# Transposing the softmax weights as 32-bit words on the matrix engine of a cached attention kernel

## The chip, the cores and the metric

The kernel runs on one core of a Trainium2 chip. A core has a matrix engine (TensorE, PE in the profile, with its weight loads shown apart as PEld), a vector engine (VectorE, DVE), a scalar engine (ScalarE, ACT), GpSimd (POOL) and a sync engine (SyncE, SP), which here only issues DMAs. Each engine works through its own list of instructions in order; engines wait for one another on semaphores. Matrix results land in PSUM (eight banks of 128 partitions by 512 fp32 words), everything else lies in SBUF. The metric is the device time of one execution, in microseconds. The kernel before takes 455.86 us, the median of three runs.

## What is computed

```python
B, Sq, D = 8, 112, 640
H, Sk, Dh = 32, 512, 192
q = (x @ wq).reshape(B, Sq, H, Dh).transpose(0, 2, 1, 3)
scores = einsum("bhqd,bhkd->bhqk", q, k_cache) * Dh ** -0.5
p = softmax(scores, axis=-1)
o = einsum("bhqk,bhkd->bhqd", p, v_cache)
out = o.transpose(0, 2, 1, 3).reshape(B, Sq, H * Dh) @ wo
```

All inputs are bf16. There are 8 x 32 = 256 pairs of a batch entry and a head; each has a 112 x 512 score matrix, and p of each has to be turned round (keys on partitions) before it can be multiplied with v.

## The kernel before, in words

A **step** n treats four heads of one batch entry; there are 64 steps, numbered 0 to 63. `t = n // 4` is a pair of half (16 heads) and batch entry. In step n the matrix engine computes scores for n (`scores`, the matmuls named `Sm` and `St`, lines 368 to 383, into banks 0 to 3), multiplies p with v for step n-2 (`values`, `PVt` line 459 and `PVm` line 470, banks 4 and 5), does a share of the query projection for a later step (`q_fill`, line 313: `Qa` is 10 matmuls of 224 columns into bank 6, `Qb` is 5), a share of the output projection of an earlier group of heads (`o_half`, line 504, bank 7: 12 matmuls of 224 columns for one block of outputs, 24 for two), and transposes p of step n-1 (`transposes`, line 431, `PT`, 8 transposes into bank 4 and 8 into bank 5).

The softmax of one head: DVE scales and negates the scores from PSUM into `s_sb` and takes the row minimum at once (`smax`, line 396; `s_sb` has two slots, so the third `smax` of a step waits for the first `exp`), ACT exponentiates into `p_sb` with the row sum (`exp`, line 401), DVE inverts two row sums (`rc`, line 413) and scales p (`norm`, line 405). After the transposes of step n-1, ACT copies bank 4 and DVE copies bank 5 to `pT_sb` (`evPT`, line 437). ACT also copies the result of p times v (`evPV`, line 480) and the projected queries (`evQa` and `evQb`, line 319). DVE also copies queries to a second layout (`qc`, lines 345 and 346) and adds the output projection to its sum (`oacc`, lines 520 and 522).

The order on every engine is written out by hand: a loop over n from 4 to 57 (lines 732 to 773) appends the operations of each step to the lists `pe`, `act` and `dve`, and lists at the start and the end (`go`, `TAIL`) do so for the rest. `Plan.run` emits each list in order and waits on a semaphore only for those dependencies that the engine has not yet seen. What sets the start of an operation is thus its place in the list of its engine, and the dependencies given to `add`. A dependency that matters here is made in `fill`: the first operation that writes a PSUM bank waits for the copy that last emptied it, so `PT(n-1)` waits for `evPV(n-2)`, since both use banks 4 and 5.

In step n the lists are:

- PE: scores(n), p times v (n-2), `Qa`, output projection part 0, `PT(n-1)`, output projection part 1, `Qb`. With one block of outputs, part 0 has 8 of 12 matmuls; with two blocks 12 of 24. Where a step has no query projection (n = 18 and 19, "light"), all but the last matmul count as part 0 and both parts lie ahead of `PT`.
- ACT: `exp` 0, `exp` 1, `evPV(n-2)`, `exp` 2, `evQa`, `exp` 3, `evPT(n-1, 0)`, `evQb`.
- DVE: `smax` 0 to 3, `rc` 0, `norm` 0 and 1, `qc(n+1)`, `evPT(n-1, 1)`, `oacc`, `rc` 1, `norm` 2 and 3. In light steps `qc` lies after `smax` 1.

The output projection goes round in four steps: n = 16, 20, 24, ... has one block, 17, 21, 25, ... two, the next two one each. Steps 9, 10, 13 and 14 have such shares too, steps 11 and 15 two shares each; steps 4 to 8 and 12 have none. Steps 57 to 61 get their p turned round by DMA (`BY_DMA`, line 418) and not on PE; `transposes` is used for 59 steps.

On SP one list issues all loads: for each t, k by a transposing DMA (line 150, waits for the scores of t-2), v for the second eight heads of t-1 (line 165, waits until its buffer has been used), weights now and then (`wo` at line 208, `wq` at line 198), v for the first eight heads of t.

Of the kernel before, what the change touches and what calls it, by code (L numbers as in the profile page):

```python
# [11 lines left out]
class Plan:  # L12
# [7 lines left out]
    def add(self, eng, name, deps, emit, sem=None, inc=1):  # L20
        assert name not in self.ops, name
        self.ops[name] = dict(eng=eng, deps=deps, emit=emit, sem=sem or eng, inc=inc)

    def number(self):
        self.count = {}
        for eng, names in self.order.items():
            for n in names:
                o = self.ops[n]
                o["at"] = {}
                for s in o["sem"] if isinstance(o["sem"], tuple) else (o["sem"],):  # L30
                    self.count[s] = self.count.get(s, 0) + o["inc"]
                    o["at"][s] = self.count[s]
        assert sum(map(len, self.order.values())) == len(self.ops)

    def run(self, eng_name, eng, sems):
        seen = {}
        for n in self.order[eng_name]:
            o = self.ops[n]
            need = {}
            for d in o["deps"]:  # L40
                if d in self.ops:
                    for s, v in self.ops[d]["at"].items():
                        need[s] = max(need.get(s, 0), v)
            for s, v in need.items():
                if seen.get(s, 0) < v:
                    eng.wait_ge(sems[s], v)
                    seen[s] = v
            last = o["emit"](eng)
            for ins, s in zip(last if isinstance(last, tuple) else (last,), o["at"]):
                ins.then_inc(sems[s], o["inc"])  # L50


def build_mha_kernel(nc, x, k_cache, v_cache, wq, wo, out):
# [27 lines left out]
    with ExitStack() as es:  # L81
# [15 lines left out]
        ident = sb("ident", [128, 128], BF16)  # L97
        nmx = sb("nmx", [SQ, 8], F32)
# [206 lines left out]
        def q_fill(m, lp, part, bank):  # L305
            half, bp = divmod(m, B // 2)
            blocks = (0, 1) if part == "a" else (2,)

            def emit(e):
                for j, c in enumerate(blocks):  # L310
                    for dc in range(DC):
                        c0 = lp * 2 * DH + 128 * c
                        mm = e.matmul(ps[:, bank, j * S2:(j + 1) * S2], wq_sb[:, dc, c0:c0 + 128],  # L313
                                      xT_sb[:, dc, bp * S2:(bp + 1) * S2], start=(dc == 0), stop=(dc == DC - 1))
                return mm

            def evac(e):
                n = len(blocks)
                return e.activation(q_home(m, lp)[:, blocks[0]:blocks[0] + n, :],  # L319
                                    ps[:, bank, 0:n * S2].rearrange("p (c s) -> p c s", c=n), ACTF.Copy)  # L320

            old = []
            if m != 1 and q_seq.index((m, lp)) >= NQ:
                for n in q_last(*q_seq[q_seq.index((m, lp)) - NQ]):
                    old += [("St", n, 3), ("qc", n)]
            rows = range(bp * S2 // 128, (bp * S2 + S2 - 1) // 128 + 1)
            add("PE", ("Q" + part, m, lp), [wq_piece[half, lp]] + [("evX", c) for c in rows], emit)
            add("ACT", ("evQ" + part, m, lp), [("Q" + part, m, lp)] + old, evac)
# [59 lines left out]
        def softmax(n):  # L388
            for i in range(4):
                j, h = divmod(i, 2)  # L390
                k = (4 * n + i) % 8
                a = (4 * n + i) % NSS
                old = divmod(4 * n + i - NSS, 4)

                def smax(e, j=j, h=h, k=k, a=a):
                    return e.tensor_scalar(s_sb[:, a, :].rearrange("p (e c) -> p e c", e=2),  # L396
                                           ps[0:SQ, 2 * j:2 * j + 2, h * 256:(h + 1) * 256], -scale, None,
                                           op0=ALU.mult, op1=ALU.min, accum_out=nmx[:, k:k + 1])

                def exp(e, k=k, a=a):  # L400
                    return e.activation(p_sb[:, k, :], s_sb[:, a, :], ACTF.Exp, bias=nmx[:, k:k + 1], scale=-1.0,  # L401
                                        accum_out=rsum[:, k:k + 1])

                def norm(e, k=k):
                    return e.tensor_scalar(p_sb[:, k, :], p_sb[:, k, :], rinv[:, k:k + 1], None, op0=ALU.mult)  # L405
                add("DVE", ("smax", n, i), [("St", n, 2 * j + 1), ("exp", *old)], smax)
                add("ACT", ("exp", n, i), [("smax", n, i), ("TD", n - 2) if n - 2 in BY_DMA else ("PT", n - 2, j)], exp)
                add("DVE", ("norm", n, i), [("rc", n, j)], norm)
# [15 lines left out]
        def transposes(n, j):  # L424
            bank = end_bank.get(("PT", n, j), 4 + j)

            def emit(e):
                for h in range(2):
                    for q in range(4):
                        c = (4 * h + q) * SQ  # L430
                        mm = e.transpose(psb[:, bank, c:c + SQ], p_sb[:, (4 * n + 2 * j + h) % 8, q * 128:(q + 1) * 128],  # L431
                                         ident[0:SQ, 0:SQ])
                return mm

            def evac(e):
# [3 lines left out]
                ([("smax", n, i) for i in range(4)] if n == NN - 1 else []), emit)  # L439
            add("DVE" if j else "ACT", ("evPT", n, j), [("PT", n, j)] + ([] if n - 1 in BY_DMA else [("PVm", n - 1, j)]), evac)  # L440

        def values(n):
# [5 lines left out]
            def pT(j, h, q):  # L448
# [3 lines left out]
                return pT_sb[:, j, h, q * SQ:(q + 1) * SQ]  # L452
# [32 lines left out]
        FILLS = [(0,), (1, 2), (3,), (4,)]  # L485
        KU = KB // 2
# [8 lines left out]
        def o_half(u, f, part):  # L495
# [3 lines left out]
            cut = len(todo) - 1 if (u, f) in whole else 2 * KU // 3 if len(blocks) == 1 else KU  # L499
            todo = todo[:cut] if part == 0 else todo[cut:]  # L500

            def emit(e):
                for j, m, k in todo:
                    mm = e.matmul(ps[:, o_bank(u, f), j * S2:(j + 1) * S2], wo_sb[:, KU * (u % 2) + k, m * 128:(m + 1) * 128],  # L504
                                  oT_sb[:, u % NO, k, :], start=(k == 0), stop=(k == KU - 1))
                return mm
# [3 lines left out]
            add("PE", ("O", u, f, part), deps, emit)  # L510
# [101 lines left out]
        whole = [o for n, os_ in o_at.items() for o in os_ if n not in q_at]  # L612
# [31 lines left out]
        holder = {}  # L644

        def fill(op, bank, evac, first=True):

            if op not in pe:
# [83 lines left out]
        for n in range(4, END):  # L732
# [3 lines left out]
            s_pe(n)  # L736
            late = any((place(n + 1)[0] // 2, 2 * place(n + 1)[1] + j) in qs for j in range(2))
# [9 lines left out]
            for o in os_[:1]:  # L747
                o_pe(o, 0)
                if two or light:
                    o_pe(o, 1)  # L750
            pt_pe(n - 1)
# [3 lines left out]
            elif os_ and not light:  # L755
                o_pe(os_[0], 1)
            b_q = []
            for g in qs:
                if os_:
                    q_pe(g, "b", 6)  # L760
                b_q.append(("evQb", *g))

# [6 lines left out]
            dve += [("qc", n + 1)] if not late and not early else []  # L769
            dve += [("evPT", n - 1, 1)]  # L770
            dve += [("oacc", *o) for o in (os_[1:2] if two else os_[:1])]
            dve += [("rc", n, 1), ("norm", n, 2), ("norm", n, 3)]
# [45 lines left out]
        def _(e):  # L818
            e.wait_ge(gINIT, 1)
# [20 lines left out]
        def _(e):  # L840
# [3 lines left out]
                            pattern=[[-1, 128]], channel_multiplier=1).then_inc(gINIT, 1)  # L844
    return nc
# [40 lines left out]
```

## Time and profile before

| what | value |
|---|---|
| time, median of 3 runs (lowest, highest) | 455.86 us (455.81, 456.63) |
| profiled execution, first to last instruction | 456.1 us |
| PE busy | 432.3 us, 95% |
| DVE busy | 364.6 us, 80% |
| ACT busy | 334.1 us, 73% |
| POOL busy | 0.7 us |
| mean granted clock of PE | 0.993 |
| transposes of p on PE | 944, busy 57.2 us |

For the profiled execution the page gives its span, from the first to the last instruction, and no other time; that span is 0.24 us above the median of the runs and lies between their lowest and highest. In a line of the profile the engine and the line of the code are followed by what is written, `<-`, and what is read. Brackets at the end of a line give the idle time of the engine ahead of it and who ended it. "x16" is a count of like instructions taken together; the time beside them then runs from the first start to the last end. A matmul's own length holds its way through the array, so the pace of a row of them is read from start to start.

### The profile page before, as it was taken

What the parts mean: (1) busy time and instruction counts of PE and PEld (TensorE: products, weight loads), DVE (VectorE), ACT (ScalarE), POOL (GpSimd) and SP (SyncE); (2) the same over time, 40 slices, a digit from 0 to 9 for tenths busy, and PEclk for the clock granted to TensorE, in tenths of its full rate; (3) what the DMA queues carried; (4) which work ended last, traced back from release to release, by engine and by line L of the source; (5) the groups of instructions that cost most, each with busy time, mean ns of one, the idle gap of its engine ahead of it and who ended that gap; (6) DMA issues with size and microseconds to landing.
All of it is one profiled execution on the core that took longest, in us unless ns stands there. A gap on an engine that the chain in (4) does not pass through costs nothing.

```text
span 456.1 us, 14769 instructions
## 1 busy us (share of the span) xinstructions
PE 432.3 (95%) x6227; PEld 398.1 (87%) x6227; DVE 364.6 (80%) x1160; ACT 334.1 (73%) x782; POOL 0.7 (0%) x6
## 2 busy tenths in 40 slices
PE   5788999999979999999999999997999999999996
PEld 4777888989979899999999999996999999999996
DVE  0577799888868989888888888886688888889971
ACT  3668799867857777877687768776577687767783
POOL 0000000000000000000000000000000000000000
PEclk9999999999999999999999999998899999999999
DMA  8999999999999999999999999999989999999972
GB/s 266 373 363 202 284 244 374 216 314 313 245 317 230 345 230 316 243 293 276 253 319 239 315 228 334 282 235 367 226 225 262 261 213 250 270 225 251 225 204 64
DMA packets 243442, 121.93 MB, mean 267 GB/s; under 512 B 194864, under 2 KB 243376, under 8 KB 243376
## 3 DMA queue, kind: packets, MB, share of 16 engines
q1 hardware_dynamic: 243376, 120.99, 110.0%
q8 instruction: 49, 0.80, 0.7%
q14 instruction: 17, 0.14, 0.1%
HBM read 70.35 MB, written 1.15 MB: 157 GB/s over the span
## 4 chain that ended last, share of the span: by engine, by line
PE 79%; ACT 10%; DMA 6%; DVE 5%; issue 0%; SPq 0%; DVEq 0%
PE ps L504 17%; PE ps L313 16%; PE ps L470 10%; PE ps L431 9%; PE ps L381 7%; ACT p_sb L401 6%; PE ps L459 6%; PE ps L368 6%; PE ps L370 5%; DMA wo_sb<-in_wo_dram 3%; DVE s_sb L396 2%; DMA vt<-in_v_cache_dram 2%; PE ps L543 1%; ACT oT_sb L480 1%; PE ps L567 1%; DVE p_sb L405 1%
## 5 line engine op out<-in xcount | busy, mean ns | idle before, releaser
L401 ACT ACTIVATE p_sb<-s_sb,nmx 112x512 bf16<-112x512 f32 x256 | 182.4, 713 | 83.8 <-DVE s_sb L396 81.8
L396 DVE TENSOR_SCALAR_CACHE_REDUCE s_sb<-ps 112x512 f32<-112x512 f32 x256 | 167.2, 687 | 42.5 <-ACT p_sb L401 20.0
L313 PE MATMUL ps<-xT_sb,wq_sb 128*128 128x224 bf16 x960 | 111.4, 262 | 1.3 <-ACT xT_sb L278 1.3
L504 PE MATMUL ps<-oT_sb,wo_sb 128*128 128x224 bf16 x840 | 97.7, 261 | 3.3 <-DMA wo_sb<-in_wo_dram 3.3
L313 PEld LDWEIGHTS ps<-xT_sb,wq_sb 128*128 128x128 bf16 x960 | 90.2, 99 | 2.8 <-DMA wq_sb<-in_wq_dram 1.1
L405 DVE TENSOR_SCALAR p_sb<-p_sb,rinv 112x512 bf16<-112x512 bf16 x256 | 79.0, 350 | 4.4
L504 PEld LDWEIGHTS ps<-oT_sb,wo_sb 128*128 128x128 bf16 x840 | 78.8, 98 | 3.9 <-DMA wo_sb<-in_wo_dram 3.6
L319 ACT ACTIVATE qr<-ps 128x448 bf16<-128x448 f32 (+1 forms) x112 | 48.9, 441 | 16.1 <-PE ps L313 16.0
L431 PE MATMUL ps<-ident,p_sb 112*128 112x112 bf16 x944 | 57.2, 214 | 1.9 <-ACT oT_sb L480 1.9
L437 ACT ACTIVATE pT_sb<-ps 128x896 bf16<-128x896 bf16 x59 | 53.3, 903 | 4.4 <-PE ps L431 3.7
L431 PEld LDWEIGHTS ps<-ident,p_sb 112*128 112x128 bf16 x944 | 52.0, 99 | 4.1 <-ACT oT_sb L480 4.1
L470 PE MATMUL ps<-pT_sb,vt 128*128 128x112 bf16 x880 | 52.8, 213 | 0.0
L480 ACT ACTIVATE oT_sb<-ps 128x672 bf16<-128x672 f32 x64 | 45.4, 710 | 6.0 <-PE ps L470 6.0
L401 ACT ACTIVATION_READ_ACCUMULATOR p_sb<-s_sb,nmx 112x1 f32 x256 | 48.4, 189 | 0.0
L470 PEld LDWEIGHTS ps<-pT_sb,vt 128*128 128x128 bf16 x880 | 44.1, 98 | 4.3
L437 DVE COPY pT_sb<-ps 128x896 bf16<-128x896 bf16 x59 | 36.4, 616 | 9.1 <-PE ps L431 9.0
L459 PEld LDWEIGHTS ps<-pT_sb,vt 128*64 128x64 bf16 x880 | 24.0, 109 | 14.2 <-issue 9.5
L459 PE MATMUL ps<-pT_sb,vt 128*64 128x112 bf16 x880 | 32.1, 216 | 4.2 <-DVE s_sb L396 2.4
L370 PE MATMUL ps<-kt,qh 128*112 128x256 bf16 x128 | 35.2, 275 | 0.0
L368 PE MATMUL ps<-kt,qh 128*112 128x256 bf16 x128 | 35.1, 274 | 0.0
L368 PE MATMUL ps<-kt,qr 128*112 128x256 bf16 x112 | 31.0, 277 | 3.8 <-DVE qh L346 2.3
L383 PE MATMUL ps<-kt,qh 64*112 64x256 bf16 x128 | 34.0, 291 | 0.0
(70 smaller groups left out, 481.3 us busy)
## 6 DMA issues: line engine op xcount, KB each, us to landing
vt<-in_v_cache_dram SPq DMA_DIRECT2D x30, 1536.0 KB, 8.6
wo_sb<-in_wo_dram SPq DMA_DIRECT2D x4, 1920.0 KB, 13.0
wq_sb<-in_wq_dram SPq DMA_DIRECT2D x7, 960.0 KB, 11.2
wo_sb<-in_k_cache_dram SPq DMA_DIRECT2D x2, 768.0 KB, 10.2
wo_sb<-in_k_cache_dram SPq DMA_DIRECT2D x1, 1536.0 KB, 15.0
wo_sb<-in_v_cache_dram SPq DMA_DIRECT2D x1, 1536.0 KB, 7.8
wq_sb<-in_v_cache_dram SPq DMA_DIRECT2D x1, 1536.0 KB, 8.1
out_dram<-xT_sb SPq DMA_DIRECT2D x8, 140.0 KB, 2.3
```

What stands on the lines that cost most here:

```text
L313: mm = e.matmul(ps[:, bank, j * S2:(j + 1) * S2], wq_sb[:, dc, c0:c0 + 128], xT_sb[:, dc, bp * S2:(bp + 1) * S2], start=(dc == 0), stop=(d ...
L368: e.matmul(ps[0:SQ, 2 * j, hs], ev, ktb[:, :, 0, cs(i)], start=(h == 0), stop=False, skip_group_check=True)
L370: mm = e.matmul(ps[0:SQ, 2 * j + 1, hs], od, ktb[:, :, 2, cs(i)], start=(h == 0), stop=False, skip_group_check=True)
L396: return e.tensor_scalar(s_sb[:, a, :].rearrange("p (e c) -> p e c", e=2), ps[0:SQ, 2 * j:2 * j + 2, h * 256:(h + 1) * 256], -scale, None, ...
L401: return e.activation(p_sb[:, k, :], s_sb[:, a, :], ACTF.Exp, bias=nmx[:, k:k + 1], scale=-1.0, accum_out=rsum[:, k:k + 1])
L405: return e.tensor_scalar(p_sb[:, k, :], p_sb[:, k, :], rinv[:, k:k + 1], None, op0=ALU.mult)
L431: mm = e.transpose(psb[:, bank, c:c + SQ], p_sb[:, (4 * n + 2 * j + h) % 8, q * 128:(q + 1) * 128], ident[0:SQ, 0:SQ])
L437: return e.activation(dst, src, ACTF.Copy) if j == 0 else e.tensor_copy(dst, src)
L459: mm = e.matmul(ps[64 * h:64 * h + 64, b0 + j, SQ:2 * SQ], vtb[:, h0 + 2 * j + h, d0:d0 + 64], pT(j, h, q), start=(q == 0), stop=(q == 3))
L470: mm = e.matmul(ps[:, b0 + j, 2 * h * SQ:(2 * h + 1) * SQ], vtb[:, h0 + 2 * j + h, d0:d0 + 128], pT(j, h, q), start=(q == 0), stop=(q == 3))
L480: return e.activation(dst.rearrange("p (j c) s -> p j c s", j=2), ps[:, b0:b0 + 2, 0:3 * SQ].rearrange("p j (c s) -> p j c s", c=3), ACTF. ...
L504: mm = e.matmul(ps[:, o_bank(u, f), j * S2:(j + 1) * S2], wo_sb[:, KU * (u % 2) + k, m * 128:(m + 1) * 128], oT_sb[:, u % NO, k, :], start ...
```

## The change

Two neighbouring bf16 values of p, of keys 2c and 2c+1, are read as one 32-bit word. A transpose then takes 112 queries by 128 words, 256 keys; two of them do a head in place of four. Their result is 128 partitions by 112 words, and each partition holds, query by query, the two keys of a word side by side. To make the keys come out in an order that fits v, `smax` writes the even and the odd half of the scores interleaved into `s_sb` (for the steps that are transposed by DMA it stays as it was), and the matmuls of p times v read every second bf16 value of `pT_sb`. A second identity matrix, fp32 of 112 x 112, is made at the start by POOL. The copies out of PSUM move the same bytes as before.

The order changes too. In every step with one share of output projection ("mixed": n = 9, 10, 13, 14 and 16 to 57) only two of its matmuls stay ahead of the transposes. The 8 transposes and all that followed them (10 or 22 matmuls of the output projection, 5 of `Qb`) are issued in turns, evenly spread by their number; operations whose instructions are spread like this are Python generators, and an operation waits ahead of its first instruction and signals with its last. In mixed steps DVE does `rc` 1 and `norm` 2 and 3 ahead of `evPT(n-1, 1)`. Everything else on ACT, DVE and SP stays.

```diff
+    def turns(self, lanes):
+        at = []
+        for i, lane in enumerate(lanes):
+            total = sum(self.ops[n]["n"] for n in lane)
+            k = 0
+            for n in lane:
+                for j in range(self.ops[n]["n"]):
+                    at.append(((k + 0.5) / total, i, n, j))
+                    k += 1
+        return [(n, j) for _, _, n, j in sorted(at, key=lambda a: a[:2])]
...
+            if first:
...
+                        eng.wait_ge(sems[s], v)
+                        seen[s] = v
+                going[n] = o["emit"](eng)
+            last = next(going[n]) if hasattr(going[n], "__next__") else going[n]
+            if final:
+                for ins, s in zip(last if isinstance(last, tuple) else (last,), o["at"]):
+                    ins.then_inc(sems[s], o["inc"])
...
+        identw = sb("identw", [SQ, SQ], F32)
...
                 def smax(e, j=j, h=h, k=k, a=a):
-                    return e.tensor_scalar(s_sb[:, a, :].rearrange("p (e c) -> p e c", e=2),
+                    to = "p (e c) -> p e c" if n in BY_DMA else "p (c e) -> p e c"
+                    return e.tensor_scalar(s_sb[:, a, :].rearrange(to, e=2),
...
                 for h in range(2):
-                    for q in range(4):
-                        c = (4 * h + q) * SQ
-                        mm = e.transpose(psb[:, bank, c:c + SQ], p_sb[:, (4 * n + 2 * j + h) % 8, q * 128:(q + 1) * 128],
-                                         ident[0:SQ, 0:SQ])
-                return mm
+                    for a in range(2):
+                        c = (2 * h + a) * SQ
+                        yield e.transpose(ps[:, bank, c:c + SQ],
+                                          p_sb[:, (4 * n + 2 * j + h) % 8, a * 256:(a + 1) * 256].bitcast(F32), identw[:, :])
...
-                return pT_sb[:, j, h, q * SQ:(q + 1) * SQ]
+                a, odd = q % 2, q // 2
+                return pT_sb[:, j, h, a * S2:(a + 1) * S2].rearrange("p (s e) -> p s e", e=2)[:, :, odd]
...
+        CUT = 2
...
-            cut = len(todo) - 1 if (u, f) in whole else 2 * KU // 3 if len(blocks) == 1 else KU
-            todo = todo[:cut] if part == 0 else todo[cut:]
+            todo = todo[:CUT] if part == 0 else todo[CUT:]
...
+            mixed = bool(os_) and not two
...
             for o in os_[:1]:
                 o_pe(o, 0)
-                if two or light:
+                if two:
                     o_pe(o, 1)
+            at = len(pe)
             pt_pe(n - 1)
...
-            elif os_ and not light:
+            elif os_:
                 o_pe(os_[0], 1)
...
+            if mixed:
+                pe[at:] = [("turns", [pe[at:at + 2], pe[at + 2:]])]
...
+            second = [("rc", n, 1), ("norm", n, 2), ("norm", n, 3)]
+            dve += second if mixed else []
             dve += [("evPT", n - 1, 1)]
             dve += [("oacc", *o) for o in (os_[1:2] if two else os_[:1])]
-            dve += [("rc", n, 1), ("norm", n, 2), ("norm", n, 3)]
+            dve += [] if mixed else second
...
-            e.wait_ge(gINIT, 1)
+            e.wait_ge(gINIT, 2)
...
+            e.memset(identw[:], 0.0).then_inc(gI0, 1)
+            e.wait_ge(gI0, 2)
+            e.affine_select(out=identw[:], in_=identw[:], compare_op=ALU.not_equal, fill=1.0, base=0,
+                            pattern=[[-1, SQ]], channel_multiplier=1).then_inc(gINIT, 1)
```

## The prediction

> **What bounds the kernel now.** I read the page's first part, then the groups with shapes kept apart, then the timeline of one step engine by engine, then the chain that ended last. The page says that PE is the fullest engine:
>
> ```profile
> PE 432.3 (95%) x6227; PEld 398.1 (87%) x6227; DVE 364.6 (80%) x1160; ACT 334.1 (73%) x782; POOL 0.7 (0%) x6
> ```
>
> Busy shares are averages, so I took one step with one block of output projection (n = 27 and the start of 28), on PE:
>
> ```profile
> 203.18 0.93 PE L504 MATMUL ps<-oT_sb,wo_sb 128*128 128x224 bf16 x8
> 203.94 0.95 PE L431 MATMUL ps<-ident,p_sb 112*128 112x112 bf16 x16
> 204.73 0.55 PE L504 MATMUL ps<-oT_sb,wo_sb 128*128 128x224 bf16 x4
> 205.12 0.64 PE L313 MATMUL ps<-xT_sb,wq_sb 128*128 128x224 bf16 x5
> ```
>
> Start to start, 16 transposes take 0.79 us (49 ns each), a matmul of 224 columns 96 ns. PE never idles here; such a step is 6.23 us long, one with two blocks 7.38 us. So transposes are on the path. But DVE is nearly as full in the same step:
>
> ```profile
> 200.92 0.69 DVE L396 TENSOR_SCALAR_CACHE_REDUCE s_sb<-ps 112x512 f32<-112x512 f32 x1
> ...
> 202.62 0.69 DVE L396 TENSOR_SCALAR_CACHE_REDUCE s_sb<-ps 112x512 f32<-112x512 f32 x1 [0.40 <-ACT p_sb L401]
> ...
> 204.04 0.61 DVE L405 TENSOR_SCALAR p_sb<-p_sb,rinv 112x512 bf16<-112x512 bf16 x2
> 204.69 0.33 DVE L345 COPY qh<-qr 64x672 bf16<-64x672 bf16 x1
> ...
> 205.28 0.61 DVE L437 COPY pT_sb<-ps 128x896 bf16<-128x896 bf16 x1
> 205.82 0.38 DVE L520 COPY accT<-ps 128x224 f32<-128x224 f32 x1
> 206.22 0.17 DVE L413 RECIPROCAL rinv<-rsum 112x2 f32<-112x2 f32 x1
> 206.42 0.62 DVE L405 TENSOR_SCALAR p_sb<-p_sb,rinv 112x512 bf16<-112x512 bf16 x2
> 207.15 0.69 DVE L396 TENSOR_SCALAR_CACHE_REDUCE s_sb<-ps 112x512 f32<-112x512 f32 x1
> ```
>
> From the first `smax` to the next step's is 6.23 us. DVE's only wait is 0.40 (`smax` 2 on `exp` 0), and 0.11 us lie open at the end (207.04 to 207.15). And ACT, which feeds DVE and frees PE's banks:
>
> ```profile
> 203.08 0.71 ACT L480 ACTIVATE oT_sb<-ps 128x672 bf16<-128x672 f32 x1
> ...
> 204.82 0.72 ACT L401 ACTIVATE p_sb<-s_sb,nmx 112x512 bf16<-112x512 f32 x1
> ```
>
> The last is `exp` 3, 3.90 us after `smax` 0. How the bank wait looks when it binds is seen in a light step, whose `smax` 0 started at 144.00; how `rc` follows an `exp` that began at 436.95, near the end:
>
> ```profile
> 146.92 0.96 PE L431 MATMUL ps<-ident,p_sb 112*128 112x112 bf16 x16 [0.31 <-ACT oT_sb L480]
> ```
> ```profile
> 437.78 0.17 DVE L413 RECIPROCAL rinv<-rsum 112x2 f32<-112x2 f32 x1 [0.65 <-ACT p_sb L401]
> ```
>
> So transposes can start 2.92 us after `smax` 0 at the earliest, and `rc` 0.83 us after its `exp` began.
>
> **The change, part by part.** Times below are from `smax` 0 of a step.
>
> *DVE's new order.* `rc` 1 now lies ahead of `evPT` and `oacc`. DVE gets there at 4.36 (205.28), but `exp` 3 lets it go at 3.90 + 0.83 = 4.73: a new wait of 0.37 us that the two copies filled before. Then `rc` 0.20 (206.22 to 206.42), two `norm` 0.65 (204.04 to 204.69), `evPT` 0.54, `oacc` 0.40 (205.28, 205.82, 206.22): the next `smax` 0 at 6.52. Queued behind the waiting `rc` are `evPT(n-1, 1)`, for which p times v of the next step waits, and that next `smax`, for which ACT waits. So a one-block step takes at least 6.52 us by DVE, 0.29 more than now. Had `evPT` stayed ahead it would wait instead for the last transpose, which now comes near the end of the turns.
>
> *PE's step.* Only 2 of the output matmuls, and by the spacing 1 (one block) or 2 (two) of the turns, lie ahead of the first transpose. PE would be there 0.4 to 0.7 us earlier than now, but `evPV` frees the bank only at 2.92, so it stalls there, with the rest of the turns behind it: 14 matmuls of 224 columns (1.34 us) or 25 (2.40), and 8 transposes; then scores until the next `smax` 0, 1.55 us (193.13 to 194.68). What is saved on transposes is thus partly given to the stall.
>
> *A transpose of words.* No row has one. Bounds: below, the bf16 one of the same 112 columns, 49 ns; above, four passes of it, 198 ns. I take the row whose load is of the plainer kind:
>
> ```profile
> L431 PEld LDWEIGHTS ps<-ident,p_sb 112*128 112x128 bf16 x944 | 52.0, 99 | 4.1 <-ACT oT_sb L480 4.1
> L592 PEld LDWEIGHTS ps<-ident,accT 128*112 128x112 bf16 x40 | 2.8, 131 | 0.7 <-DVE accT L576 0.4 <-issue 0.4
> ```
>
> L592's loads are longer (131 against 99 ns), and its five transposes of 128 columns run at some 57 ns each (0.45 us together, the last one 0.22). The turns with 224-column matmuls give each load some 96 ns of cover; without it the load would show. The Trainium skill's "TensorE: Matmul & The Clock Gate", sections Terms and Weight-path perf modes, says that trn2's transpose mode makes fp32 four times faster, but that fast weight load is off for fp32; the first would put a transpose at the 49 ns end, the second speaks against the change and for the row taken, and no run so far shows an fp32 load. With 57 ns: one block 2.92 + 1.34 + 0.46 + 1.55 = 6.27, hidden under DVE's 6.52; two blocks 2.92 + 2.40 + 0.46 + 1.55 = 7.33 against 7.38 now.
>
> *Strided operands.* `smax` writes every second word. Nearest are the additions of line 522: 391 ns to fp32 in a row, 410 ns to every second bf16; I take half of those 19 ns for the one `smax` in the loop, 0.4 us over 44 steps (ends 0 and, scaled to 512 elements, 1.9). p times v reads every second bf16. Loads with that stride (L592) take 131 ns, as those of 112 columns in a row do (line 368, 131 ns): nothing, or at worst half speed, 1.3 us a step, of which 0.4 lies under the stall. The second identity costs POOL some 0.5 us after 1.5 us; PE waits for x until 4.46 anyway: nothing.
>
> *Steps.* Mixed are 31 steps of one block with `Q`, 13 of two, 2 light. One block: 31 x 0.29 = +9.0. Two: 13 x (-0.05) = -0.7. Light: `exp` 3 at 3.48 (147.48), `rc` at 4.31, then 0.20 + 0.65 + 0.54 + 0.40, so 6.10 against 5.55 now (144.73 to 150.28), +1.1. In steps 4 to 8 and 12 chains of `exp` or a v load bind; steps 11 and 15 gain 0.4 on PE, but the p times v after each waits for v (up to 101.82 and 130.37): nothing. The end: 4 instead of 8 transposes ahead of the last copy, -0.2.
>
> *A stall that shrinks.* This one is bound by a DMA that was issued behind a k load and does not follow the pace of the steps:
>
> ```profile
> 317.22 1.67 PE L504 MATMUL ps<-oT_sb,wo_sb 128*128 128x224 bf16 x8 [3.33 <-DMA wo_sb<-in_wo_dram]
> ```
>
> The last step that set a time in that chain of DMAs is five steps back (v at 280.65); four one-block steps and one of two will be 1.1 us longer, so the wait falls to 2.2: -1.1. After it 8 matmuls took 1.67 us where 8 take 0.77: the granted clock was 0.51 from 317.2 to 323.4, and the step lost 0.90 + 0.70 + 0.37 + 0.45 + 0.66 = 3.1 us. After the wait of 2.40 us at 130.37 it was 1.00. With 2.2 I expect it to stay: -3.1. The skill's page named above (section Part 1, the HAM clock gate) puts the fall after an idle window of some 3.4 us; both rows agree.
>
> Sum: 9.0 - 0.7 + 1.1 - 0.2 - 1.1 - 3.1 + 0.4 = **+5.4 us**. It is made on the profiled execution, whose span is 456.1; I add it to the median, 455.86: 461.3 us.
>
> **Rivals.**
> - *The clock falls all the same* (windows may start anywhere, and the wait may come out nearer 3.3): without the 3.1, 464.4 us.
> - *A word costs what two bf16 transposes do*, 99 ns, so that the change doesn't save PE what it says. For: twice the bytes. Then PE binds, 2.92 + 1.34 + 0.79 + 1.55 = 6.60 and 7.66: 31 x 0.37 + 13 x 0.28 + 1.1 - 1.8 - 3.1 + 0.4 = +11.7, 467.6 us.
> - *Four passes (198 ns), or half speed of p times v*: 7.39 and 8.45, light 6.91: 36 + 14 + 3, less 6 for the stall: 503 us; p times v at half speed comes near it (+0.9 a step, some 495).
> - *Faster*: ACT's chain isn't the limit. Place: `rc` 1 on DVE. If `exp` 3 frees it by 4.36 instead of 4.73, and `evPV` frees the banks as much sooner, one-block steps fall to DVE's 6.12 (-0.11) and two-block ones by the whole 0.40: 31 x 0.11 + 13 x 0.40 = -8.6, some 448 us with the longer wait for wo. Against: ACT's list is not touched, and from `smax` 0 to `exp` 3 it has no gap in this step.
> - *Gains and losses cancel*: the 0.37 us wait half as long (`exp` 3 a little sooner) and the clock kept: 455 to 457 us.
>
> **How the numbers follow.** The forecast has 0.36, the fallen clock 0.20, two bf16's price 0.16, the four passes 0.13, faster 0.10, cancelled 0.05. By themselves the likeliest's bounds are 459 to 463.5 (49 ns a transpose, -0.9; strided `smax` +1.5). The range goes from 455 to 478: it leaves out the four passes and most of the faster case. Within 0.2% is 454.9 to 456.8, about what a measurement of this kernel can tell from no change: faster 0.10, same 0.05, slower 0.85.
>
> **What would show it.** On DVE, `rc` (line 413) waits some 0.37 us for `exp` in about 44 steps, 16 us in all, and `evPT` and `oacc` follow `norm`. On PE, transposes stall on `evPV` in nearly every mixed step, and one-block steps are 6.5 us apart, two-block ones 7.3. Eight transposes are spread among the 224-column matmuls; how much longer the turns are than those alone is their price, 0.46 us by mine. At the wo load the idle is near 2.2 us and the clock stays. The prediction is wrong if a word's transpose costs over 90 ns, if p times v gets slower than 0.52 + 0.80 us, or if DVE doesn't wait at `rc` 1.

## The result

The changed kernel takes 468.82 us (median of four runs, 468.52 to 470.06) against 455.84 us for the kernel before in the same session (454.99 to 456.63): a ratio of 1.0293, 95% interval 1.0270 to 1.0317, or 13.0 us slower. The forecast was 461.3 us, 5.4 us slower.

The page of the changed kernel: the busy times, the chain that ended last, and the groups of the new transposes (busy us, mean ns of one | idle before them).

```profile
PE 441.2 (94%) x5755; PEld 396.9 (85%) x5755; DVE 365.4 (78%) x1160; ACT 334.0 (71%) x782; POOL 1.1 (0%) x8
...
PE 55%; ACT 29%; DVE 11%; DMA 4%; issue 1%
...
L462 PE MATMUL ps<-identw,p_sb 112*128 112x112 f32 x472 | 108.1, 266 | 9.7 <-ACT oT_sb L511 8.7
...
L462 PEld LDWEIGHTS ps<-identw,p_sb 112*128 112x128 f32 x472 | 61.6, 140 | 22.5 <-ACT oT_sb L511 21.8
```

PE has 472 instructions fewer and is busy 9 us longer. Its share of the chain fell (before: PE 79%, ACT 10%) and ACT's rose: PE now stands behind `evPV` (line 511 here), which itself follows `exp` 0 and `exp` 1. The waits say the same (us in all, times, longest):

```profile
DVE s_sb L427 <- PE ps L413: 23.4, 54, 2.2
PEld ps L462 <- ACT oT_sb L511: 21.8, 48, 1.4
...
DVE rinv L444 <- ACT p_sb L432: 17.0, 51, 1.0
...
PE ps L462 <- ACT oT_sb L511: 8.7, 34, 1.1
```

The first weight load of a step's transposes waits for `evPV` 48 times, and there are 46 mixed steps. `rc` (line 444) waits 17.0 us for `exp`; the forecast had 16. And `smax` waits for the scores of PE 54 times (before: 24). So DVE is not what ends a step last, PE is. One step with one block of output projection, on PE:

```profile
201.65 0.45 PE L535 MATMUL ps<-oT_sb,wo_sb 128*128 128x224 bf16 x3
202.28 0.32 PE L462 MATMUL ps<-identw,p_sb 112*128 112x112 f32 x1 [0.18 <-ACT oT_sb L511]
202.43 0.36 PE L535 MATMUL ps<-oT_sb,wo_sb 128*128 128x224 bf16 x2
202.62 0.26 PE L462 MATMUL ps<-identw,p_sb 112*128 112x112 f32 x1
202.72 0.35 PE L535 MATMUL ps<-oT_sb,wo_sb 128*128 128x224 bf16 x2
...
204.48 0.27 PE L398 MATMUL ps<-kt,qr 128*112 128x256 bf16 x1
```

and on DVE, from the step's first `smax` to the next:

```profile
199.35 0.69 DVE L427 TENSOR_SCALAR_CACHE_REDUCE s_sb<-ps 112x512 f32<-112x512 f32 x1 [0.39 <-PE ps L413]
...
204.09 0.17 DVE L444 RECIPROCAL rinv<-rsum 112x2 f32<-112x2 f32 x1 [0.29 <-ACT p_sb L432]
...
205.36 0.38 DVE L551 COPY accT<-ps 128x224 f32<-128x224 f32 x1
206.03 0.69 DVE L427 TENSOR_SCALAR_CACHE_REDUCE s_sb<-ps 112x512 f32<-112x512 f32 x1 [0.29 <-PE ps L413]
```

The bank comes free 2.93 us after `smax` 0 (202.28); then come 14 matmuls of 224 columns (1.34 us) and eight words (0.86 us) until scores at 204.48, and 1.55 us of scores: 6.68 us, where this step took 6.23. From 202.62 to 202.72 one word costs 0.10 us, as much as a matmul of 224 columns; only the first one, behind the wait, takes 0.15 (202.28 to 202.43). At the end DVE waits 0.29 us for PE. Steps of two blocks take 7.72 us (7.38 before), light ones 6.20 (5.55).

Where the time is, in the two profiled executions: 31 x 0.45 + 13 x 0.34 + 2 x 0.65 = +19.7; the wait for wo (3.33 us before) is gone, -3.3; the granted clock is 1.000 throughout (0.993 before), -3.1. That makes +13.3. The two spans, 456.1 and 468.2, are 12.1 us apart. The remaining -1.2 are three other waits for loads: for v near 130 us (2.40 us before, 1.13 now), for v near 102 us (1.11 and 1.78) and for x at the start (4.5 and 3.9). Such waits differ from one execution of a program to the next: in the experiment that only adds matmuls behind the changed kernel's end, the wait near 130 us is 2.43 us and not 1.13. So the +19.7 of the steps belong to the change, and the rest of this sum to these two executions. Nor is 456.1 a device time: wherever both are on record, the device time is 1.7 to 1.9 us above the span, so the profiled execution of the kernel before took some 457.9 us, about 2 us more than the median and more than the highest of the runs.

### The profile page after: what moved, and what is told of

The parts are those of the page before. It is cut to its first block, busy times and chain, and to the rows that moved or that the text cites. A ratio compares the mean times of both kernels' runs of the same rounds, so it can differ in the third digit from the quotient of the medians.

```text
span 468.2 us, 13828 instructions
## 1 busy us (share of the span) xinstructions
PE 441.2 (94%) x5755; PEld 396.9 (85%) x5755; DVE 365.4 (78%) x1160; ACT 334.0 (71%) x782; POOL 1.1 (0%) x8
## 4 chain that ended last, share of the span: by engine, by line
PE 55%; ACT 29%; DVE 11%; DMA 4%; issue 1%
ACT p_sb L432 20%; PE ps L535 13%; PE ps L462 10%; DVE s_sb L427 8%; ACT oT_sb L511 7%; PE ps L344 7%; PE ps L411 6%; PE ps L398 5%; PE ps L400 5%; DMA vt<-in_v_cache_dram 3%; PE ps L501 2%; PE ps L490 1%; PE ps L574 1%; PE ps L598 1%; DVE p_sb L436 1%
## 5 line engine op out<-in xcount | busy, mean ns | idle before, releaser
L344 PE MATMUL ps<-xT_sb,wq_sb 128*128 128x224 bf16 x960 | 118.5, 261 | 1.3 <-ACT xT_sb L309 1.3
L462 PE MATMUL ps<-identw,p_sb 112*128 112x112 f32 x472 | 108.1, 266 | 9.7 <-ACT oT_sb L511 8.7
L535 PE MATMUL ps<-oT_sb,wo_sb 128*128 128x224 bf16 x840 | 117.2, 259 | 0.0
L535 PEld LDWEIGHTS ps<-oT_sb,wo_sb 128*128 128x128 bf16 x840 | 83.8, 101 | 0.2
L462 PEld LDWEIGHTS ps<-identw,p_sb 112*128 112x128 f32 x472 | 61.6, 140 | 22.5 <-ACT oT_sb L511 21.8
L501 PE MATMUL ps<-pT_sb,vt 128*128 128x112 bf16 x880 | 54.4, 213 | 0.0
L501 PEld LDWEIGHTS ps<-pT_sb,vt 128*128 128x128 bf16 x880 | 45.5, 96 | 4.4
L444 DVE RECIPROCAL rinv<-rsum 112x2 f32<-112x2 f32 x128 | 20.9, 163 | 18.0 <-ACT p_sb L432 17.0
```

The lines of the kernel that those rows point to most:

```text
L344: yield e.matmul(ps[:, bank, j * S2:(j + 1) * S2], wq_sb[:, dc, c0:c0 + 128], xT_sb[:, dc, bp * S2:(bp + 1) * S2], start=(dc == 0), stop=( ...
L462: yield e.transpose(ps[:, bank, c:c + SQ], p_sb[:, (4 * n + 2 * j + h) % 8, a * 256:(a + 1) * 256].bitcast(F32), identw[:, :])
L501: mm = e.matmul(ps[:, b0 + j, 2 * h * SQ:(2 * h + 1) * SQ], vtb[:, h0 + 2 * j + h, d0:d0 + 128], pT(j, h, q), start=(q == 0), stop=(q == 3))
L535: yield e.matmul(ps[:, o_bank(u, f), j * S2:(j + 1) * S2], wo_sb[:, KU * (u % 2) + k, m * 128:(m + 1) * 128], oT_sb[:, u % NO, k, :], star ...
```

## The experiments

Two theories stood at the start. A: what costs is the order, since with only two or four matmuls ahead of them the transposes and all that is issued behind them hang on the bank that `evPV` frees, so that nothing of PE's work lies under that wait any more. B: what costs is the word, as dear as two bf16 transposes. The sessions' own medians for the kernel before were 457.74 us (the first four experiments), 457.94 (the next four) and 456.94 (the last two).

| run | us | ratio to before [95%] |
|---|---|---|
| the changed order, bf16 transposes | 474.4 | 1.0404 [1.0348, 1.0460] |
| the order of before, words | 455.9 | 0.9971 [0.9931, 1.0011] |
| the changed kernel, early share restored | 462.5 | 1.0143 [1.0054, 1.0232] |
| the changed kernel, DVE's order restored | 483.0 | 1.0557 [1.0505, 1.0609] |
| the changed order, half of the transposes | 456.6 | 0.9993 [0.9955, 1.0031] |
| before, wo in two loads | 455.0 | 0.9970 [0.9937, 1.0004] |
| the order of before, words, wo in two loads | 454.7 | 0.9946 [0.9910, 0.9981] |
| the changed kernel, bank freed sooner | 458.5 | 1.0052 [1.0015, 1.0089] |
| the changed kernel, early share restored, `evQa` first | 457.2 | 0.9991 [0.9957, 1.0024] |

### The order without the words

```diff
-                    for a in range(2):
-                        c = (2 * h + a) * SQ
-                        yield e.transpose(ps[:, bank, c:c + SQ],
-                                          p_sb[:, (4 * n + 2 * j + h) % 8, a * 256:(a + 1) * 256].bitcast(F32), identw[:, :])
+                    for q in range(4):
+                        c = (4 * h + q) * SQ
+                        yield e.transpose(psb[:, bank, c:c + SQ], p_sb[:, (4 * n + 2 * j + h) % 8, q * 128:(q + 1) * 128],
+                                          ident[0:SQ, 0:SQ])
```

`smax` and p times v go back to their strides of before with it; 16 bf16 transposes a step are spread among the matmuls.

> Theory A (the order costs the time: the transposes stall on the bank that evPV frees 2.93 us after the first smax of a step, and all that was moved behind them follows; words as such save nothing): with 16 bf16 transposes of 49 ns in the place of the 8 words, and all else as in the changed kernel, a one-block step is 2.93 + 15 x 0.096 + 0.79 + 1.55 = 6.71 us (the changed kernel 6.68), a two-block step 2.93 + 26 x 0.096 + 0.79 + 1.55 = 7.77 (7.72): 467 to 471 us. Theory B (the words are what costs, the order is harmless): 454 to 458 us.

Measured 474.4 us, even above the changed kernel, three over A's range and far from B's. PE in one step:

```profile
187.94 0.26 PE L534 MATMUL ps<-oT_sb,wo_sb 128*128 128x224 bf16 x1
188.51 0.22 PE L462 MATMUL ps<-ident,p_sb 112*128 112x112 bf16 x1 [0.31 <-ACT oT_sb L510]
188.57 0.26 PE L534 MATMUL ps<-oT_sb,wo_sb 128*128 128x224 bf16 x1
188.67 0.21 PE L462 MATMUL ps<-ident,p_sb 112*128 112x112 bf16 x1
188.72 0.26 PE L534 MATMUL ps<-oT_sb,wo_sb 128*128 128x224 bf16 x1
```

The same stall, and a pair of a transpose and a matmul takes 0.15 us (188.57 to 188.72), as the two would apart (0.049 + 0.096). Turns as such cost little: the 16 transposes and 15 matmuls from 188.51 to the scores at 190.82 come to 54 ns a transpose instead of 49, some 0.08 us a step, and with that the step is 6.79 us and not 6.71. The order makes the kernel slow without any word in it.

### The words without the order

```diff
-                    for q in range(4):
-                        c = (4 * h + q) * SQ
-                        mm = e.transpose(psb[:, bank, c:c + SQ], p_sb[:, (4 * n + 2 * j + h) % 8, q * 128:(q + 1) * 128],
-                                         ident[0:SQ, 0:SQ])
+                    for a in range(2):
+                        c = (2 * h + a) * SQ
+                        mm = e.transpose(ps[:, bank, c:c + SQ],
+                                         p_sb[:, (4 * n + 2 * j + h) % 8, a * 256:(a + 1) * 256].bitcast(F32), identw[:, :])
```

This is the kernel before with the word transposes, the interleaved `smax` and the strided p times v; every list stays in its old order.

> Words alone, every engine's order as in the kernel before. Theory A: eight words at 0.103 us are 0.82 us where sixteen bf16 transposes are 0.79, p times v reads with a step at +0.03 us a step, so +0.06 us in some 50 steps that PE binds: 457 to 460 us. Theory B: 466 to 470 us. A third, that the load of a word shows unless other matmuls cover it: eight in a row take over 1.0 us instead of 0.82, and 470 us or more.

Measured 455.9 us, not to be told from before (the interval of the ratio is 0.4% to either side), just below A's range and far from the other two. One-block steps take 6.25 us, two-block ones 7.40, each 0.02 more than before. PE in such a step:

```profile
181.94 0.93 PE L507 MATMUL ps<-oT_sb,wo_sb 128*128 128x224 bf16 x8
182.71 0.93 PE L433 MATMUL ps<-identw,p_sb 112*128 112x112 f32 x8
183.48 0.55 PE L507 MATMUL ps<-oT_sb,wo_sb 128*128 128x224 bf16 x4
```

Eight words take 0.77 us (182.71 to 183.48), eight matmuls of 224 columns as long (181.94 to 182.71). The 16 bf16 transposes of before took 0.79. So the load doesn't show even where no other matmul covers it. By themselves the words neither cost nor save.

### The price of a word, by itself

```diff
             P.run("PE", e, sems)
+            words = p_sb[:, 0, 0:256].bitcast(F32)
+            for i in range(64):
+                e.transpose(ps[:, 0, 0:SQ], words, identw[:, :])
+            for i in range(64):
+                e.transpose(ps[:, 0, 0:72], words[0:72], identw[0:72, 0:72])
+            for i in range(64):
+                e.transpose(ps[0:72, 0, 0:SQ], words[:, 0:72], identw[:, :])
...
+            for i in range(64):
+                e.matmul(ps[:, 0, 0:S2], wo_sb[:, 0, 0:128], oT_sb[:, 0, 0, :], start=True, stop=True)
```

At the end of the changed kernel PE does six groups of 64 instructions in a row; two of bf16 transposes (left out above) lie between the third and the last. Its one execution, 499.1 us, isn't compared with the others.

> The changed kernel with six groups of 64 matmuls each behind its last work on PE, whose results nobody reads: words 112 x 128 through 112 columns; words of 72 rows (72 moving columns, 128 loaded); words with 72 loaded columns (112 moving); bf16 112 x 128; bf16 with 72 loaded columns; and an ordinary bf16 matmul of 224 columns. If the moving fp32 columns set a word's price (two column times each): some 100 ns, 65 ns, 100 ns, 49 ns, 49 ns, 96 ns, start to start. If the load of fp32 sets it: some 100, 100, 60 to 65, and the rest the same.

The groups (busy us of all 64, the last one's own length included, then mean ns of one):

```profile
L861 PE MATMUL ps<-identw,p_sb 112*128 112x112 f32 x64 | 6.3, 259 | 0.0
L865 PE MATMUL ps<-identw,p_sb 112*72 112x112 f32 x64 | 6.3, 259 | 0.0
L871 PE MATMUL ps<-oT_sb,wo_sb 128*128 128x224 bf16 x64 | 6.3, 259 | 0.0
L861 PEld LDWEIGHTS ps<-identw,p_sb 112*128 112x128 f32 x64 | 6.1, 140 | 0.0
...
L863 PE MATMUL ps<-identw,p_sb 72*128 72x72 f32 x64 | 4.2, 227 | 0.0
...
L867 PE MATMUL ps<-ident,p_sb 112*128 112x112 bf16 x64 | 3.3, 213 | 0.0
```

From the start of one group to that of the next, divided by 64 (the first runs from 468.16 to 474.30), a word transpose takes 96 ns with 112 moving columns, whether 128 or 72 words are loaded; 63 ns with 72 moving columns; a bf16 one 49 ns with 112; a bf16 matmul of 224 columns 96 ns. So a moving column of fp32 takes the time of two bf16 columns, and the longer weight load (140 ns) is hidden behind that. Eight words can't take less than 0.77 us; B's price is right, though the run before this one shows that it is no loss by itself.

### The early share of matmuls, restored

```diff
-            todo = todo[:CUT] if part == 0 else todo[CUT:]
+            cut = 2 * KU // 3 if len(blocks) == 1 else KU
+            todo = todo[:cut] if part == 0 else todo[cut:]
```

The changed kernel with 8 (or 12) matmuls ahead of the transposes again, which are then spread among the rest.

> The changed kernel, but 8 of 12 (or 12 of 24) matmuls of the output projection lie ahead of the transposes again; words, turns and DVE's order stay. Theory A: the transposes come 3.15 us after the first smax, later than the bank's 2.93, so no stall; PE's one-block step is 6.33 us and DVE's loop through exp 3 binds at 6.42 (the copies' last start 205.36 less 199.35, and 0.41 to the next smax), two-block steps 7.47: 458 to 462 us. If the stall on the bank is not what costs: 467 to 470 us.

Measured 462.5 us, half a microsecond above A's range: half of the loss is back. The stall on the bank is gone from these steps (one block 6.51 us, two blocks 7.43), but another has come. PE where `Qb` begins, and the wait in all:

```profile
198.38 0.26 PE L536 MATMUL ps<-oT_sb,wo_sb 128*128 128x224 bf16 x1
198.48 0.26 PE L462 MATMUL ps<-identw,p_sb 112*128 112x112 f32 x1
198.79 0.27 PE L344 MATMUL ps<-xT_sb,wq_sb 128*128 128x224 bf16 x1
```
```profile
PEld ps L344 <- ACT qr L349: 7.5, 29, 0.4
```

`Qb` writes bank 6, which `evQa` empties, and `evQa` lies behind `exp` 2 on ACT. With most output matmuls ahead again, four of them and half of the words are all that lies between the first word and `Qb`, so PE gets there some 0.2 us before the copy is done. Whether this wait was all that was left is tried last.

### DVE's order, restored

```diff
             second = [("rc", n, 1), ("norm", n, 2), ("norm", n, 3)]
-            dve += second if mixed else []
             dve += [("evPT", n - 1, 1)]
             dve += [("oacc", *o) for o in (os_[1:2] if two else os_[:1])]
-            dve += [] if mixed else second
+            dve += second
```

> The changed kernel, but DVE has its old order: evPT(n-1, 1) and oacc ahead of rc 1 and the two norms. The last transposed word now comes 5.2 us after the first smax of a one-block step (6.1 in a two-block one). Theory A (DVE is a second bound through whatever it waits for): evPT waits for it, then 0.53 + 0.40 + 0.20 + 0.65 follow: one-block steps 7.0 us and two-block 8.2, 480 to 487 us. Theory B (PE alone is the bound, DVE's order is free): 467 to 470 us.

Measured 483.0 us, as expected: `evPT` now waits on DVE for the last word of the turns.

```profile
DVE pT_sb L467 <- PE ps L462: 49.6, 48, 1.7
```

One-block steps take 6.90 us, two-block ones 8.09. Given the turns, the new order on DVE is no loss: by the two ratios (1.0557 and 1.0293) it saves some 12 us. Its wait for `exp` 3 at `rc` 1 is real, but PE ends the step later still.

### The changed order with half of the transposes

```diff
-                    for a in range(2):
+                    for q in range(2):
...
-                        yield e.transpose(ps[:, bank, c:c + SQ],
-                                          p_sb[:, (4 * n + 2 * j + h) % 8, a * 256:(a + 1) * 256].bitcast(F32), identw[:, :])
+                        yield e.transpose(psb[:, bank, c:c + SQ], p_sb[:, (4 * n + 2 * j + h) % 8, q * 128:(q + 1) * 128],
+                                          ident[0:SQ, 0:SQ])
```

Eight bf16 transposes a step at some 50 ns in the places of the eight words: only the first half of each head's keys is transposed, and `evPT` writes that half twice, with as many bytes as before. The strides of `smax` and of p times v go too. It is the changed kernel near the price that the forecast had assumed (57 ns), and it asks if DVE's loop is then 6.52 us.

> The changed order with 8 bf16 transposes a step in the place of the 8 words, 49 ns each; half of the keys are left out (the copies read each transposed block twice and move as many bytes as before). It gives the transposes the price that the prediction had. If that price was its one error: PE's one-block step is 2.93 + 1.34 + 0.42 + 1.55 = 6.24 us and DVE's loop of 6.51 binds, two-block steps 7.30: 4 to 8 us above the kernel before. If DVE's loop doesn't bind: one-block steps of 6.25 us, and no more than 1 us above before. If something else in the changed order costs: as the changed kernel, 11 us or more above.

Measured 456.6 us, level with before; so the number is that of the case in which DVE's loop doesn't bind. DVE in a one-block step:

```profile
182.52 0.68 DVE L427 TENSOR_SCALAR_CACHE_REDUCE s_sb<-ps 112x512 f32<-112x512 f32 x1
...
187.25 0.17 DVE L444 RECIPROCAL rinv<-rsum 112x2 f32<-112x2 f32 x1 [0.30 <-ACT p_sb L432]
187.45 0.62 DVE L436 TENSOR_SCALAR p_sb<-p_sb,rinv 112x512 bf16<-112x512 bf16 x2
187.98 0.62 DVE L468 COPY pT_sb<-ps 128x896 bf16<-128x896 bf16 x1
188.51 0.38 DVE L551 COPY accT<-ps 128x224 f32<-128x224 f32 x1
188.81 0.68 DVE L427 TENSOR_SCALAR_CACHE_REDUCE s_sb<-ps 112x512 f32<-112x512 f32 x1
```

DVE does bind here: after `rc` 1 it waits for nothing until the next `smax`. But its loop is 6.29 us long. `rc` starts at 4.73, to the hundredth as forecast; from there it is 0.20 + 0.53 + 0.53 + 0.30 = 1.56 us to `smax`, not 0.20 + 0.65 + 0.54 + 0.40 = 1.79. The 0.65 had been read where `qc` follows the two `norm`s; `evPT` follows them after 0.53. The 0.40 had been read where `rc` follows `oacc`; `smax` follows it after 0.30.

### The load of wo in two parts

```diff
+            ks = [(0, 8), (8, KB // 2)] if (half, u) == (1, 1) else [(0, KB // 2)]
+            for i, (k0, k1) in enumerate(ks):
+                def emit(e, k0=k0, k1=k1):
...
+            if part == 1 and f == 0 and (half, u % 2) == (1, 1):
+                deps = [("WO2", 1, 1)]
```

The kernel before, with the one load of wo for which PE waited 3.33 us cut in 8 and 4 blocks of rows; the last four matmuls alone wait for the second. It asks what the wait, and the slow clock behind it, were worth. The second run does the same to the kernel with words in the old order.

> The kernel before with the one wo load that PE waits for cut in two DMAs (8 and 4 of 12 row blocks), the first half of the output projection waiting for the first only. If the wait and the clock after it cost what the prediction says (3.3 us idle, 3.1 us at half clock): the idle falls to 0 to 2 us, the clock stays at 1.00, and the kernel is 3 to 6 us faster than before. If the stall is made up later by other waits: within 1 us of before.

> The same cut of the wo load, on the kernel with words in the old order. If words are free: as the cut load on the kernel before, within 1.5 us, 3 to 6 us faster than before.

Measured 455.0 and 454.7 us. The wait for wo in the first, in all:

```profile
PE ps L506 <- DMA wo_sb<-in_wo_dram: 0.3, 1, 0.3
```

By the medians they are 2.9 and 3.3 us below before, by the ratios 1.4 and 2.5: at the low end of the 3 to 6 us that were expected, or under it. The first one's interval takes in 1; the second's does not, and it is the one version here that is shown to be faster than the kernel before, by 0.2 to 0.9%. What the wait and the slow clock were worth can't be read cleanly from the first. The idle fell as expected, and the step that held it went from 12.62 to 6.75 us. But the clock didn't stay at 1.00: it fell to 0.50 from 131.67 to 135.08 us, behind a wait of 2.29 us for v, and the step there took 10.24 us instead of 8.70.

### The bank freed sooner

```diff
+            moved = mixed and not late and not early
...
-            act += [("exp", n, 0), ("exp", n, 1)] + [("evPV", n - 2)]
+            if moved:
+                act += [("exp", n, 0), ("evPV", n - 2), ("exp", n, 1)]
+            else:
+                act += [("exp", n, 0), ("exp", n, 1)] + [("evPV", n - 2)]
```

The changed kernel with PE's list as it is. Only ACT's copy of p times v comes ahead of `exp` 1, and DVE's `qc` fills the gap that this makes between `smax` 2 and 3.

> The changed kernel with the stall on the bank taken away from the other side: ScalarE copies the bank of p times v out (evPV) directly behind exp 0 of a mixed step, instead of behind exp 1, so that the bank comes free some 0.6 us sooner, and VectorE puts the copy of the queries (qc) between smax 2 and smax 3, where it would otherwise wait for the later exp 1. TensorE's list stays as it is, with two or four matmuls ahead of the transposes. Theory A (what a mixed step lost beyond the words' own time is that everything behind the bank's release stands on the loop): the stall of 0.18 to 0.31 us goes, the first word no longer costs 0.26 to 0.32 us alone; a one-block step 6.40 to 6.50 instead of 6.68, a two-block one 7.45 to 7.55 instead of 7.72; 44 steps by 0.2 to 0.28 are 9 to 12 us: 456 to 460 us. Rival B (the turns of words and matmuls are slow by themselves, whatever stands ahead): the transposes start sooner and the step ends when it did: 466 to 470 us.

Measured 458.5 us, in A's range. PE at the first word (the step's `smax` 0 is at 178.10), then DVE:

```profile
180.39 0.45 PE L535 MATMUL ps<-oT_sb,wo_sb 128*128 128x224 bf16 x3
180.68 0.26 PE L462 MATMUL ps<-identw,p_sb 112*128 112x112 f32 x1
180.78 0.35 PE L535 MATMUL ps<-oT_sb,wo_sb 128*128 128x224 bf16 x2
```
```profile
178.10 0.69 DVE L427 TENSOR_SCALAR_CACHE_REDUCE s_sb<-ps 112x512 f32<-112x512 f32 x1
...
182.94 0.17 DVE L444 RECIPROCAL rinv<-rsum 112x2 f32<-112x2 f32 x1 [0.28 <-ACT p_sb L432]
...
184.50 0.69 DVE L427 TENSOR_SCALAR_CACHE_REDUCE s_sb<-ps 112x512 f32<-112x512 f32 x1
```

The first word starts at 2.58 instead of 2.93 with no idle ahead of it, and the step is 6.40 us long: now DVE binds, since `exp` 3 lets `rc` go at 4.84. Two-block steps take 7.43. The same words in the same turns are thus some 11 us cheaper (1.0052 against 1.0293) when the bank is free in time.

### The early share restored, and `evQa` ahead of `exp` 2

```diff
+            cut = 2 * KU // 3 if len(blocks) == 1 else KU
...
-            act += [("exp", n, 2)] + a_q + [("exp", n, 3)]
+            act += a_q + [("exp", n, 2), ("exp", n, 3)] if mixed else [("exp", n, 2)] + a_q + [("exp", n, 3)]
```

> The changed kernel with the share of 8 (12) matmuls ahead of the transposes given back, as in the run with the early share restored, and ScalarE's first copy of the queries (evQa) put ahead of exp 2, so that the second query matmuls no longer wait for that copy as they did there (0.3 us a step). Theory A (the loss of the changed kernel is the stall, and of that run what was left is the wait for evQa): both waits gone, a one-block step 6.25 to 6.35, a two-block one 7.35 to 7.45, as in the kernel before within 0.1: 455 to 459 us. Rival B (what was left in that run is the price of words in turns): no gain on that run, 461 to 465 us.

Measured 457.2 us, A's range, level with before. A one-block step on DVE:

```profile
179.53 0.69 DVE L427 TENSOR_SCALAR_CACHE_REDUCE s_sb<-ps 112x512 f32<-112x512 f32 x1
...
184.27 0.17 DVE L444 RECIPROCAL rinv<-rsum 112x2 f32<-112x2 f32 x1 [0.29 <-ACT p_sb L432]
...
185.83 0.68 DVE L427 TENSOR_SCALAR_CACHE_REDUCE s_sb<-ps 112x512 f32<-112x512 f32 x1
```

6.30 us: the stall and the wait for `evQa` are both gone, and what ends the step is DVE's loop, 0.07 above before. So the change's loss hangs on the order around the bank: with the stall away, words, turns, strides and DVE's order together are level with the old kernel. Here PE reaches its first word 3.14 us after `smax` 0, nine matmuls having gone ahead; with three, as in the changed kernel, it would be there 6 x 0.096 sooner, at 2.56. The bank comes free at 2.93, so by this reckoning the stall is worth 0.37 us a step of the 0.45 lost, though the waits show 0.18 of it as idle time of PE; the other 0.08 are mostly that eight words in turns take 0.86 us (0.77 in a row) where 16 transposes took 0.79.

## Why the prediction was wrong

It forecast a slower kernel and was 7.5 us short, and it named the wrong engine. Its +9.0 us, more than the whole forecast, came from DVE's loop through `rc` 1, under which PE's step was to be hidden; in fact PE's step through the bank's release ends last, and DVE waits 0.29 us for it.

- **A transpose of words: the step that failed.** It took 57 ns, the row of line 592, whose loads are long, so 0.46 us for eight. The price is 96 ns in a row, and eight in the turns take 0.86 us. The row was chosen for its load, but the load is hidden, in a row of words too; the columns that move set the price, and an fp32 column takes two column times. With 0.86 us for eight, the prediction's own sum for PE is 2.92 + 1.34 + 0.86 + 1.55 = 6.67 and 7.73 (measured 6.68 and 7.72): PE binds, as in the rival "a word costs what two bf16 transposes do", which gave 467.6 us (measured 468.8). The first of the prediction's own signs of being wrong, over 90 ns a word, was met. The Trainium skill's "TensorE: Matmul & The Clock Gate", section Terms, has the transpose mode make fp32 four times faster; the trace does not bear out that end, 49 ns a word, but two column times a column. The same page of the Trainium skill, section Weight-path perf modes, leaves fast weight load off for fp32; the loads are slower here (140 against 98 ns), and set no price.
- **DVE's new order.** The wait at `rc` 1 is as forecast (4.74 and 17.0 us in all, against 4.73 and 16). The loop of 6.52 was mis-sized, 6.29 measured, since steps taken from other rows were 0.23 too long. With 6.29 this term of +9.0 is +1.9. So the two errors partly made up for each other: with half of the transposes, near the forecast's own price, the kernel is level with before, where the forecast gave +5.4. That it said slower at all was thus in part luck: DVE's loop, from which it had this, costs nothing here that PE's step doesn't cover.
- **The stall on `evPV`.** Right in place, time (2.92 forecast, 2.93 measured) and number of steps. That it gives back what the transposes save was right too; the transposes save nothing, so it became the loss.
- **Strided operands.** `smax` takes 689 ns against 687. PE's main part of p times v goes from 0.80 to 0.83 us, under the stall. Both within the bounds; p times v is 0.03 us over the 0.80 that the prediction named as a sign, which costs nothing here.
- **Light steps.** 6.20 against the forecast's 6.10; +1.3 us instead of +1.1.
- **The wait for wo and the clock.** The slow clock is gone, as forecast (-3.1). The wait should have shrunk to 2.2 us; there is none. The steps on the way were longer by 4 x 0.45 + 0.34 = 2.1 us, not 1.1; that leaves 1.2 of the 3.33. One execution's wait is no firm ground for such a term: with words in the old order, whose steps are within 0.02 us of before, it is 1.89 us and not 3.33. In the other profiles it is 1.89 to 2.43 where one-block steps take 6.30 to 6.50 us, and none where they take 6.67 or more, which fits a wait that longer steps shrink; where the 1.2 went, and how far the wait differs between executions of one kernel, isn't settled.

Of the rivals, "the clock falls all the same" and "four passes, or half speed of p times v" are excluded by the granted clock of 1.000 and by 0.10 us a word; "faster" and "cancelled" by the time.

## What to carry to other kernels

Price an operation in a new type by what streams through the engine, and take a row for that, not for its load: half as many transposes of words twice as wide save nothing on PE when each word's column takes two column times. Before independent work is moved behind an operation that waits for a buffer, look when that buffer comes free: on an engine that is full, work ahead of the wait is what hides it, and each hundredth that the engine stands is a hundredth of the step. A sum of spacings around a loop needs each pair of neighbours from a row of that very pair; two tenths of error made a loop that would cost 0.06 us a step look like 0.29.

## What was not expected of the hardware

- A fp32 transpose moves a column in two bf16 column times: 96 ns for 112, 63 ns for 72, and the same for 128 or 72 words loaded.
- The granted clock can fall after a shorter idle than the prediction supposed. It stayed at 1.00 after PE had idled 2.40 us in the kernel before (at 130.37) and 1.89 us with words in the old order, but fell to 0.50 after 2.25 us where the bank was freed sooner. In the last run (early share, `evQa` first) it stayed at 1.00 even after 3.52 us of waiting for v:

```profile
106.15 0.60 PE L490 MATMUL ps<-pT_sb,vt 128*64 128x112 bf16 x16 [3.52 <-DVE rinv L444]
```

The bracket names `rc`, on which this matmul doesn't depend; the last part of the load of v landed at 106.01, 0.14 us ahead of it, as far ahead as where the bracket names the load.

PE where the bank was freed sooner:

```profile
322.34 0.46 PE L535 MATMUL ps<-oT_sb,wo_sb 128*128 128x224 bf16 x3 [2.25 <-DMA wo_sb<-in_wo_dram]
322.64 0.26 PE L462 MATMUL ps<-identw,p_sb 112*128 112x112 f32 x1
...
323.01 0.39 PE L462 MATMUL ps<-identw,p_sb 112*128 112x112 f32 x1
323.20 0.58 PE L535 MATMUL ps<-oT_sb,wo_sb 128*128 128x224 bf16 x2
```

The first matmuls behind the wait run at full speed (three in 0.30 us); the fall comes some 0.5 us later, and from 323.01 each takes 0.19 us instead of 0.10, until 326.25. The Trainium skill's "TensorE: Matmul & The Clock Gate", section Part 1 on the clock gate, asks for an idle window of some 3.4 us. The slow stretch is that long (3.42 us), but the idle ahead of it was 2.25 us only, so the prediction's "both rows agree" held for its two rows and not in general. The length of an idle alone does not tell if the clock falls, and the -3.1 us came out right in part because the wait went away altogether.
- Transposes alone keep the clock up: the five groups of 64 in a row, from 468.16 to 490.78 us in the run on the price of a word, went at a granted clock of 1.00 throughout.
